# Mean of squares in a fused attention and gated feed-forward kernel: TensorE sums replaced by VectorE 32x32 transposes, once per two head pairs

## The chip, the cores and the metric

The kernel runs on one core of a Trainium2 chip. The metric is device time in microseconds for one execution. A core has TensorE (PE in the profile, its weight loads PEld), VectorE (DVE), ScalarE (ACT), GpSimd (POOL) and SyncE (SP), which here issues nearly all DMAs. Matmuls write to PSUM, which has eight banks of 128 partitions by 512 fp32.

## The reference

Two layers, one behind the other. First a linear attention with a root-mean-square norm over each head, then a feed-forward layer with a gate:

```python
kv  = einsum('bhsd,bhse->bhde', k, v)          # batch 8, heads 8, seq 576, head_dim 64
out = einsum('bhsd,bhde->bhse', q, kv)
x   = out / sqrt(mean(out * out, axis=-1) + 1e-6) * g_norm
x   = x.transpose(0, 2, 1, 3).reshape(4608, 512)
h   = x @ w_in                                  # 512 -> 2048
sp  = maximum(h, 0) + log1p(exp(-abs(h)))       # softplus
out = (h * erf(sp)) @ w_out                     # 2048 -> 512
```

The mean of squares is over the 64 values of one head, and that sum is what the change moves.

## The kernel before, in words

**Groups.** The 4608 tokens are worked in nine groups of 512, `T` = 0 to 8. Group `T` below 8 is the first 512 rows of batch entry `T`; the last 64 rows of each entry are gathered in the tile `x_last` and make up group 8. Tokens lie along the free dimension and the features of two heads on the 128 partitions, so a group's attention output is four tiles of 128x512, one for each pair of heads (`p` = 0 to 3). The sum over one head is thus a sum over 64 partitions.

**Stages.** Groups 0 to 2 get their attention in code of their own (`first_group`, and `attention` for groups 1 and 2) beside the set-up of the weights and the feed-forward of groups 0 and 1, which ends near 235 us. Then comes the main loop over `m` (line 1318), one iteration for each four hidden units of a group; a group has 16 units and so four iterations, `b` = 0 to 3. An iteration makes four hidden products (`hidden`), then the four result products of the iteration before (`result`). In the profile both have line 773, and are told apart by the tiles: `x_forms,w_in_parts` for hidden, `w_out_parts,g_forms` for result. Each is 12 matmuls of 128x128 by 128x512: every operand is kept in three forms (high, low, both), eight matmuls go to the bank `n_ps` and four to the bank `m_ps`. A pair of banks is taken from six in rotation (`pair_of_banks`); the other two hold `at_ps`, the attention output of the pair in work. The weights' forms are read from DRAM afresh in each group (line 1019, four tiles in and four out in each iteration), into a few buffers.

**What follows a product.** A hidden product: ScalarE copies `n_ps` to `h` (line 1367), VectorE adds `m_ps` (line 743, `h<-m_ps,h`), ScalarE makes softplus (line 1372) and, for all four units, erf (line 1395); VectorE multiplies (line 1421, "the gates") and the next iteration cuts the gates into three forms (lines 703, 706, 709, `g_forms`). A result product: VectorE adds `n_ps` (line 738) and `m_ps` (line 743, `e<-m_ps,e`) to the running sum, or in the first iteration of a group writes it (line 1304).

**The attention of the next group.** While group `T` is worked, each iteration `b` does pair `b` of group `T+1`, cut into pieces that are called at places of the iteration: place 0 is its start, place 1 to 4 follow the hidden products 0 to 3, place 5 to 8 the result products 0 to 3. The order of the work on each engine is the order in which the code issues it (the schedule is by hand). `paired` handles groups 3 to 7: in even `b` (`side` 0) the piece `visit` makes the products of two pairs on TensorE (lines 579 and 610). In each iteration follow: `square` on ScalarE (line 634, out of `at_ps`), `halve` on VectorE (lines 640 and 641: the squares in a rounded high part and a low part), `mean` (two matmuls with the constant `mean_w`, lines 645 and 646, into a bank of the rotation that `next_bank` gives, then the exp and log table, Ln, Exp with scale -0.5, Square, lines 650 to 652), `norm` on VectorE (a correction step in two 128x512 instructions, lines 658 and 661, and the product with the attention output and g, line 665), and the split into three forms `x_forms` (lines 703, 706, 709). `keep` copies the 64-row rest and the next pairs' k-v products out of PSUM (lines 621, 378, 380); `turns` transposes the next two q tiles in blocks of 32x32 (line 345). Group 8 runs through `attention` in its branch for `T == B`, with the same steps (lines 486, 487, 498 to 518).

ScalarE's functions come from tables that have to be loaded: erf, exp with log, and softplus are three of them (`ACT_TABLE_LOAD`, lines 112, 115, 1395).

Of the kernel before, what the change touches and what calls it, by code (L numbers as in the profile page):

```python
# [39 lines left out]
FP32 = mybir.dt.float32  # L40
# [2 lines left out]
U32 = mybir.dt.uint32  # L43
AF = mybir.ActivationFunctionType
ALU = mybir.AluOpType
PSUM = bass.MemoryType.PSUM

EPS = 1e-6
# [7 lines left out]
FIRST = 2  # L56
SHIFT = 4096.0
SQ = 32
ORDER = """
kv0 fill0 q0 fill1 q_out0 kv_out0 result0 kv1 kv_out1 q1 square0 q_out1 mean0 log0 result1 kv2 kv_out2  # L60
root0 tail square1 again0 tail_out mean1 kv3 log1 root1 q2 again1 q3 q_out2 norm_a0 norm_b0 kv_out3 norm_c0 q_out3
# [7 lines left out]
def kernel(  # L69
# [262 lines left out]
    def halves_of(t):  # L332
        return t.rearrange("p (a t) -> p a t", a=2)
# [65 lines left out]
        kept.pop()()  # L399
        turn(1, 0)  # L400

    def attention(T, p, in_parts=False):

        st = {}

        halves = T > 1 or (T == 1 and p > 0)
        quad = T < B
# [4 lines left out]
        def two(t):  # L412
            return halves_of(t) if quad else t

        bd = kv_of(T, p)

        def bank(name):
            if p == 0:
                at_pool(2)
            return ps_now[0].tile([P, G], FP32, name=name, tag="at")  # L420

        def square_tile(name):
            return qt_tile(name)[:, 0:G]
# [1 line left out]
        def visit():  # L425


            qT = ready.pop((T, p))
            at = st["at"] = at_tile()
            x = halves_of(qT[:, 0:G])  # L430
            for a, i in ((0, 0), (0, 1), (1, 0), (1, 1)):
                nc.tensor.matmul(  # L432
                    at[rows_of[i if a else 1 - i], a, 0 : 2 * P],
                    lhsT=bd[rows_of[i], a * D : (a + 1) * D],
                    rhs=x[rows_of[i], a],
                    start=True,
                    stop=True,
                )
# [5 lines left out]
            if then[0] < B:  # L444
                for _, product_ in kv_products(*then, at[:, 1, kv_cols], at[:, 0, kv_cols], first=1):
                    product_()  # L446
            if both:
                for _, product_ in kv_products(then[0], 1, at[:, 1, more_cols], at[:, 0, more_cols]):
                    product_()
            st["sq"] = qT[:, 0:G]  # L450
            nc.scalar.activation(two(st["sq"]), st["o"], AF.Square)

        def keep_tail():
            nc.vector.tensor_copy(
                out=x_last[:, p, T * R : T * R + R], in_=st["at"][:, 1, 2 * P : 2 * P + R]
            )
            if then[0] < B:
                kv_kept(*then, st["at"])
            if both:
                kv_kept(then[0], 1, st["at"], more_cols)  # L460

        def square():
            st["o"], st["sq"] = x_last[:, p, :], square_tile("sq")
            nc.scalar.activation(st["sq"], st["o"], AF.Square)

        def halve():
            sq = st.pop("sq")
# [3 lines left out]
            nc.vector.tensor_tensor(out=lo, in0=sq, in1=hi.bitcast(FP32), op=ALU.subtract)  # L471

        def mean(table=True):
            if quad:
                ms = st["at"][:, :, 2 * P : 4 * P]
                parts = [(ms[:, a], a) for a in range(2)]
            else:
                ms = bank("ms_ps")
                parts = [(ms, slice(0, G))]
            st["ms"] = ms  # L480
            if halves:


# [63 lines left out]
            if i == (FIRST + 1) * NP:  # L547
                load_kv(i + 1)

        after = (split_upper, split_lower) if in_parts else (split,)  # L550
        if T == B:
            return lambda: None, square, halve, mean, norm, *after
# [4 lines left out]
        return (*(partial(chain, *group) for group in pieces), mean, partial(chain, norm, then_), *after)  # L557


    twice = {}  # L560

    def paired(T, p, in_parts=False):

        i = T * NP + p
        u_tile = partial(attp.tile, [P, G], FP32, name="u", tag="sq_lo")
        side = p % 2
        if side == 0:
            twice.clear()
        st = {}

        def visit():

# [56 lines left out]
                )  # L629

        def square():
            st["o"] = twice["at"][:, :, side * 2 * P : (side + 1) * 2 * P]
            st["sq"] = x_new.tile([P, G], FP32, name="sq", tag="x")
            nc.scalar.activation(halves_of(st["sq"]), st["o"], AF.Square)

        def halve():
            sq = st.pop("sq")
            hi = st["hi"] = attp.tile([P, G], FP32R, name="sq_hi", tag="rms_r")
            lo = st["lo"] = attp.tile([P, G], FP32R, name="sq_lo", tag="sq_lo")
            nc.vector.tensor_copy(out=hi, in_=sq)  # L640
            nc.vector.tensor_tensor(out=lo, in0=sq, in1=hi.bitcast(FP32), op=ALU.subtract)

        def mean(table=True):
            ms = st["ms"] = next_bank("ms_ps")
            nc.tensor.matmul(ms, lhsT=mean_w, rhs=st.pop("hi"), start=True, stop=False)  # L645
            nc.tensor.matmul(ms, lhsT=mean_w, rhs=st.pop("lo"), start=False, stop=True)  # L646
            u = st["u"] = u_tile()
            r = st["r"] = attp.tile([P, G], FP32, name="rms_r", tag="rms_r")
            exp_ln_table()
            nc.scalar.activation(r, ms, AF.Ln, bias=eps_col)  # L650
            nc.scalar.activation(r, r, AF.Exp, scale=-0.5)
            nc.scalar.activation(u, r, AF.Square)
            if table:
                softplus_table()

        def norm():
            ms, u, r = (st.pop(name) for name in ("ms", "u", "r"))
            nc.vector.scalar_tensor_tensor(
                out=u, in0=ms, scalar=EPS, in1=u, op0=ALU.add, op1=ALU.mult
            )  # L660
            nc.vector.scalar_tensor_tensor(
                out=u, in0=u, scalar=3.0, in1=r, op0=ALU.subtract, op1=ALU.mult
            )
            x = st["x"] = x_new.tile([P, G], FP32, name="x", tag="x")
            nc.vector.scalar_tensor_tensor(
                out=halves_of(x),
                in0=st.pop("o"),
                scalar=gm_col,
                in1=halves_of(u),
                op0=ALU.mult,  # L670
                op1=ALU.mult,
            )

        def split_upper():
            upper(st["x"], x_forms[T][0][:, p])

        def split_lower():
            lower(st.pop("x"), *(form[:, p] for form in x_forms[T]))

        def q_loads():  # L680
            if i == (FIRST + 1) * NP:
# [9 lines left out]
            for n in range(2):  # L691
                turn(*divmod(i + 1 + n, NP))

        after = (split_upper, split_lower) if in_parts else (partial(chain, split_upper, split_lower),)
        if side == 0:
            start = (q_loads, partial(chain, visit, square, halve, keep, kv_loads), chain)
        else:
            start = (chain, partial(chain, square, halve), turns)
        return (*start, mean, norm, *after)

    def upper(x, high):

# [44 lines left out]
    def pair_of_banks(*names, turns=True):  # L747
# [5 lines left out]
            banks.extend(banks[:2])  # L753
            del banks[:2]
        return pair

    def next_bank(name):
        pool, tag = banks[0]
        banks.append(banks.pop(0))
        return pool.tile([P, G], FP32, name=name, tag=tag)  # L760

    def product(weights, moving, turns=True, cuts=()):

# [554 lines left out]
    for m in range(first_batch, batches + 1):  # L1318
# [1 line left out]
        todo = []  # L1320
        last_ = b == NB - 1 and T + 1 < NG
        if T + 1 < NG:
            todo = list((attention if T + 1 == B else paired)(T + 1, b, in_parts=last_))
            if b == 0:
                side = late_r if T % 2 == FIRST % 2 else late
                forms = side.tile([P, 3, KC, G], FP32R, name=f"x_forms{(T + 1) % 2}")
                x_forms[T + 1] = [forms[:, i] for i in range(3)]

        def piece():
            if todo:  # L1330
# [12 lines left out]
        def pieces(place):  # L1343
            while todo and places[-len(todo)] <= place:
                todo.pop(0)()

        def fetch(place):
            for which in FETCH[place].split():
# [112 lines left out]
```

## Time and profile before

| what | value |
|---|---|
| median of 3 runs | 896.05 us (896.02 to 896.56) |
| the profiled execution: time | 896.7 us |
| the profiled execution: span from first to last instruction | 894.9 us |
| granted TensorE clock, mean | 1.000 |
| busy PE / PEld / DVE / ACT | 886.7 / 668.5 / 761.0 / 594.9 us |
| HBM traffic | 224.40 MB read, 34.60 MB written, 289 GB/s over the span |
| lines 645 and 646, the mean's matmuls of groups 3 to 7 | 20 each, 392 and 393 ns |
| lines 640, 641, 658, 661, 665 on DVE | 20 each, 418, 693, 684, 691, 751 ns |
| lines 650, 651, 652 on ACT | 20 each, 690, 633, 633 ns |

A row of the profile names line, engine, operation, output and inputs with their shapes, count, then busy time and the mean duration of one, and the idle time in front of it with what ended it. Durations of instructions on one engine overlap a little, so that the distance from start to start is the better price of one. Matmuls are pipelined: one takes 390 ns from its start to its end, while the next starts 227 ns behind it.

### The profile page before, as it was taken

Reading aid. Unit: us, or ns where it says so; the run is one execution under the profiler, and the core shown is the slowest. Engines: PE = TensorE matmul, PEld = TensorE weight load, DVE = VectorE, ACT = ScalarE, POOL = GpSimd, SP = SyncE. Lnnn points to the kernel's source line nnn. Section 1 sums busy time; section 2 is a strip of 40 time slices with the busy share of each in tenths; the row PEclk is TensorE's granted clock in tenths of the full one; section 3 lists DMA queues with packets and bytes.
Section 4 is the critical chain, followed back from the end, with each engine's and each line's share of the span. In section 5 each row is a group of like instructions: output and inputs, shape, how many; then the busy total and the mean of one; then the engine's idle time right before and its main releaser. Section 6 shows DMA issues by size and latency. Waiting matters only on the chain.

```text
span 894.9 us, 13333 instructions
## 1 busy us (share of the span) xinstructions
PE 886.7 (99%) x4922; PEld 668.5 (75%) x4922; DVE 761.0 (85%) x1095; ACT 594.9 (66%) x789; POOL 4.7 (1%) x14
## 2 busy tenths in 40 slices
PE   8999999999999999999999999999999999999998
PEld 4444456666788888888888888888888888888887
DVE  5899979899889898989898989898988888886667
ACT  5976677777766666666666656565666766665552
POOL 2000000000000000000000000000000000000000
PEclk9999999999999999999999999999999999999999
DMA  9977418889799987998799879998887787778861
GB/s 288 296 226 226 112 74 315 314 337 351 258 351 397 307 334 249 404 288 339 258 367 342 342 219 350 359 337 271 291 326 274 286 313 300 283 286 319 316 261 50
DMA packets 136929, 259.89 MB, mean 290 GB/s; under 512 B 78816, under 2 KB 87264, under 8 KB 136864
## 3 DMA queue, kind: packets, MB, share of 16 engines
q1 hardware_dynamic: 136128, 258.09, 81.1%
q10 hardware_dynamic: 544, 0.82, 0.3%
q8 instruction: 39, 0.64, 0.3%
q14 instruction: 26, 0.21, 0.1%
q0 software_dynamic: 192, 0.13, 0.1%
HBM read 224.40 MB, written 34.60 MB: 289 GB/s over the span
## 4 chain that ended last, share of the span: by engine, by line
PE 91%; DMA 4%; DVE 3%; ACT 2%; issue 1%; SPq 0%; DVEq 0%; ACTq 0%
PE n_ps L773 48%; PE m_ps L773 24%; PE o_ps L829 8%; PE h_ps L1196 5%; DMA w_in_parts<-w_in 1%; DMA w_out_parts<-w_out 1%; PE at_ps L579 1%; PE off_ps L610 1%; DMA w_in<-w_new 1%; PE warm_ps L977 1%; PE ms_ps L646 1%; PE ms_ps L645 1%; PE at_ps L432 0%; PE at_ps L446 0%; DMA w_out<-w_place 0%
## 5 line engine op out<-in xcount | busy, mean ns | idle before, releaser
L773 PE MATMUL n_ps<-w_out_parts,g_forms 128*128 128x512 f32 (+1 forms) x936 | 230.4, 388 | 0.3 <-DMA w_out_parts<-w_out 0.3
L773 PE MATMUL n_ps<-x_forms,w_in_parts 128*128 128x512 f32 x896 | 222.7, 391 | 0.0
L773 PEld LDWEIGHTS n_ps<-w_out_parts,g_forms 128*128 128x128 f32 x936 | 175.1, 188 | 37.2 <-DMA w_out_parts<-w_out 0.7
L773 PEld LDWEIGHTS n_ps<-x_forms,w_in_parts 128*128 128x128 f32 x896 | 167.4, 188 | 35.1
L743 DVE TENSOR_TENSOR h<-m_ps,h 128x512 f32<-128x512 f32 x116 | 78.0, 686 | 60.9 <-PE m_ps L773 57.7
L773 PE MATMUL m_ps<-w_out_parts,g_forms 128*128 128x512 f32 x464 | 123.8, 389 | 0.0
L1372 ACT ACTIVATE s<-h 128x512 f32<-128x512 f32 x112 | 69.3, 631 | 79.0 <-DVE h L743 78.9
L773 PE MATMUL m_ps<-x_forms,w_in_parts 128*128 128x512 f32 x448 | 119.7, 389 | 0.0
L1367 ACT ACTIVATE h<-n_ps 128x512 f32<-128x512 f32 x112 | 66.0, 592 | 78.3 <-PE n_ps L773 77.1
L773 PEld LDWEIGHTS m_ps<-w_out_parts,g_forms 128*128 128x128 f32 x464 | 87.1, 188 | 18.1
L773 PEld LDWEIGHTS m_ps<-x_forms,w_in_parts 128*128 128x128 f32 x448 | 84.1, 188 | 17.5
L743 DVE TENSOR_TENSOR e<-m_ps,e 128x512 f32<-128x512 f32 x116 | 80.1, 692 | 15.3 <-PE m_ps L773 5.0
L829 PE MATMUL o_ps<-w_out_sb,h_sb 128*128 128x512 f32 x192 | 86.8, 595 | 0.0
L709 DVE SCALAR_TENSOR_TENSOR g_forms<-g_forms 128x1024 fp32r<-128x1024 f32 x58 | 71.1, 1225 | 2.0
L706 DVE TENSOR_TENSOR g_forms<-h,g_forms 128x1024 fp32r<-128x1024 f32 x58 | 70.5, 1216 | 0.5 <-ACT g_forms L703 0.4
L703 ACT ACTIVATE g_forms<-h 128x1024 fp32r<-128x1024 f32 x58 | 58.4, 1049 | 15.5 <-PE m_ps L773 11.1
L738 DVE SCALAR_TENSOR_TENSOR e<-n_ps,e 128x512 f32<-128x512 f32 (+1 forms) x89 | 60.3, 678 | 7.1 <-PE n_ps L773 7.1
L1421 DVE TENSOR_TENSOR h<-h,s 128x1024 f32<-128x1024 f32 x56 | 65.9, 1217 | 0.0
L829 PEld LDWEIGHTS o_ps<-w_out_sb,h_sb 128*128 128x128 f32 x192 | 35.5, 190 | 38.3 <-issue 36.9
L1196 PE MATMUL h_ps<-xT,w_in_sb 128*128 128x512 f32 x128 | 57.9, 596 | 1.3 <-DVE w_in_sb L290 1.2
L115 ACT ACT_TABLE_LOAD x43 | 55.2, 1283 | 0.8
L1395 ACT ACTIVATE s<-s 128x1024 f32<-128x1024 f32 x50 | 50.6, 1054 | 0.3
(175 smaller groups left out, 1014.0 us busy)
## 6 DMA issues: line engine op xcount, KB each, us to landing
w_out_parts<-w_out SPq DMA_DIRECT2D x116, 768.0 KB, 7.1
w_in_parts<-w_in SPq DMA_DIRECT2D x112, 768.0 KB, 6.6
w_in<-w_new SPq DMA_DIRECT2D x16, 768.0 KB, 4.8
k_sb<-in_k_dram SPq DMA_DIRECT2D x32, 288.0 KB, 5.6
v_sb<-in_v_dram SPq DMA_DIRECT2D x31, 288.0 KB, 5.7
w_raw<-in_moe_w_in_dram SPq DMA_DIRECT2D x16, 512.0 KB, 5.9
w_raw<-in_moe_w_out_dram SPq DMA_DIRECT2D x8, 1024.0 KB, 5.0
out_dram<-e SPq DMA_DIRECT2D x32, 256.0 KB, 3.5
```

Of the source, the lines that this page charges most:

```text
L115: nc.scalar.preload_act_table_set("softplus")
L703: nc.scalar.activation(high, x, AF.Copy, scale=1.0 + 2.0**-13)
L706: nc.vector.tensor_tensor(out=low, in0=x, in1=high.bitcast(FP32), op=ALU.subtract)
L709: nc.vector.scalar_tensor_tensor(out=both, in0=low.bitcast(FP32), scalar=SHIFT, in1=high.bitcast(FP32), op0=ALU.mult, op1=ALU.add,)
L738: nc.vector.scalar_tensor_tensor(out=out_, in0=ps, scalar=scale, in1=out_, op0=ALU.mult, op1=ALU.add)
L743: nc.vector.tensor_tensor(out=out_, in0=ps, in1=out_, op=ALU.add)
L773: nc.tensor.matmul(ps[:, cols], lhsT=weights(form, k), rhs=moving(form, k)[:, cols], start=(form == forms[0] and k == 0), stop=(form == fo ...
L829: nc.tensor.matmul(o_ps[j], lhsT=g[:, j * P : j * P + P], rhs=one(w_out_sb, f), start=(f == 0), stop=last,)
L1196: nc.tensor.matmul(plain[i], lhsT=blocks_of(one(w_in_sb, i % FC))[:, c], rhs=xT[T][:, c, :], start=(c == 0), stop=(c == KC - 1),)
L1367: nc.scalar.activation(h[:, i], n_ps, AF.Copy, scale=SHIFT - 1.0)
L1372: nc.scalar.activation(s[:, i], h[:, i], AF.Softplus)
L1421: nc.vector.tensor_tensor(out=part(h, half), in0=part(h, half), in1=part(s, half), op=ALU.mult)
```

## The change

In groups 3 to 8 the mean of squares leaves TensorE. One set of pieces now serves two pairs, in even `b`: both squares are taken at once (with scale 0.125, so that the square is already divided by 64); VectorE transposes each 128x512 tile of squares in blocks of 32x32 and sums each block along the free dimension, which leaves 128x16 for a pair, 128x32 for both; ScalarE copies the four quarters of 32 partitions crosswise and VectorE adds them, since a head covers two quarters; Ln, Exp and Square run on 128x32; the correction step runs on 128x32; and a transpose of the column, read with stride 0, spreads the factor back to 128x512. The product with g follows for both pairs at place 8, the split at places 1 to 3 of the odd iteration, the transposes of the next q at its place 5 (before: place 3). `halve`, `mean` and `next_bank` are gone from this path, the exp and log table is loaded in even `b` only, and group 8 goes through the same pieces, reading `x_last`. The tiles of squares and of x are now of the tag that the transposed q has.

```diff
-    def attention(T, p, in_parts=False):
+    def attention(T, p):
...
         def square():
-            st["o"] = twice["at"][:, :, side * 2 * P : (side + 1) * 2 * P]
-            st["sq"] = x_new.tile([P, G], FP32, name="sq", tag="x")
-            nc.scalar.activation(halves_of(st["sq"]), st["o"], AF.Square)
-
-        def halve():
...
-        def mean(table=True):
-            ms = st["ms"] = next_bank("ms_ps")
-            nc.tensor.matmul(ms, lhsT=mean_w, rhs=st.pop("hi"), start=True, stop=False)
-            nc.tensor.matmul(ms, lhsT=mean_w, rhs=st.pop("lo"), start=False, stop=True)
...
+            xs = twice["x"] = [qt_tile("x")[:, 0:G] for _ in range(2)]
+            for n, x in enumerate(xs):
+                if T == B:
+                    o = x_last[:, p + n]
+                else:
+                    o, x = twice["at"][:, :, n * 2 * P : (n + 1) * 2 * P], halves_of(x)
+                twice["o", n] = o
+                nc.scalar.activation(x, o, AF.Square, scale=0.125)
+
+        def small(name):
+            t = twice[name] = attp.tile([P, 2 * BLOCKS], FP32, name=name, tag=name)
+            return t
+
+        def block_sums():
+            total = small("ms")
+            for n in range(2):
+                t = attp.tile([P, G], FP32, name="sq_t", tag=("rms_r", "sq_lo")[n])
+                nc.vector.transpose(out=t, in_=twice["x"][n])
+                nc.vector.tensor_reduce(
+                    out=total[:, n * BLOCKS : n * BLOCKS + BLOCKS],
+                    in_=t.rearrange("p (c d) -> p c d", c=BLOCKS),
+                    axis=AX.X,
+                    op=ALU.add,
+                )
+
+        def across():
+            total, other = twice["ms"], small("ms_other")
+            for n in range(4):
+                rows, beside = (slice(32 * k, 32 * k + 32) for k in (n, n ^ 1))
+                nc.scalar.copy(other[rows], total[beside])
+            nc.vector.tensor_tensor(out=total, in0=total, in1=other, op=ALU.add)
+
+        def root():
+            total, r, u = twice["ms"], small("rms"), small("rms_u")
             exp_ln_table()
-            nc.scalar.activation(r, ms, AF.Ln, bias=eps_col)
+            nc.scalar.activation(r, total, AF.Ln, bias=eps_col)
             nc.scalar.activation(r, r, AF.Exp, scale=-0.5)
             nc.scalar.activation(u, r, AF.Square)
...
+        def spread():
+            total, r, u = (twice[name] for name in ("ms", "rms", "rms_u"))
             nc.vector.scalar_tensor_tensor(
-                out=u, in0=ms, scalar=EPS, in1=u, op0=ALU.add, op1=ALU.mult
+                out=u, in0=total, scalar=EPS, in1=u, op0=ALU.add, op1=ALU.mult
             )
             nc.vector.scalar_tensor_tensor(
                 out=u, in0=u, scalar=3.0, in1=r, op0=ALU.subtract, op1=ALU.mult
             )
+            for n in range(2):
+                nc.vector.transpose(
+                    out=twice["x"][n].rearrange("p (c d) -> p c d", c=BLOCKS),
+                    in_=u[:, n * BLOCKS : n * BLOCKS + BLOCKS].unsqueeze(2).to_broadcast([P, BLOCKS, 32]),
+                )
...
         if side == 0:
-            start = (q_loads, partial(chain, visit, square, halve, keep, kv_loads), chain)
+            first = {0: (q_loads,), 2: (visit, square, keep, kv_loads)} if T < B else {0: (square,)}
+            norms = [partial(norm, n) for n in range(2)]
+            pieces = first | {3: (block_sums,), 4: (across,), 5: (root,), 6: (spread,), 8: norms}
         else:
-            start = (chain, partial(chain, square, halve), turns)
-        return (*start, mean, norm, *after)
+            pieces = {
+                1: [partial(split_upper, n) for n in range(2)],
+                2: (partial(split_lower, 0),),
+                3: (partial(split_lower, 1),),
+                5: (turns,),
+            }
+        return sorted((place, partial(chain, *some)) for place, some in pieces.items())
...
-            todo = list((attention if T + 1 == B else paired)(T + 1, b, in_parts=last_))
+            todo = paired(T + 1, b)
...
-        places = (0, 2, 3, 5, 6, 8)
-        if T + 1 == B:
-            places = (0, 0, 2, 5, 7, 8)
-        if last_:
-            places = (0, 0 if T + 1 == B else 2, 2 if T + 1 == B else 3, 4, 5, 5, 6)
-            todo[3] = partial(todo[3], table=False)
-
         def pieces(place):
-            while todo and places[-len(todo)] <= place:
-                todo.pop(0)()
+            while todo and todo[0][0] <= place:
+                todo.pop(0)[1]()
...
-            if len(todo) < 2:
+            if not last_ and (b % 2 or not todo):
                 softplus_table()
```

More of the change, by code (lines that the diff above doesn't have):

```diff
@@ L45 @@
 ALU = mybir.AluOpType
+AX = mybir.AxisListType
 PSUM = bass.MemoryType.PSUM
@@ L58 @@
 SQ = 32
+BLOCKS = 16
 ORDER = """
@@ L400, in keep_prepared @@
         turn(1, 0)
-    def attention(T, p, in_parts=False):
+    def attention(T, p):
         st = {}
         halves = T > 1 or (T == 1 and p > 0)
-        quad = T < B
         then = divmod(T * NP + p + 1, NP)
@@ L410, in attention @@
         more_cols = slice(kv_cols.stop, kv_cols.stop + D)
-        def two(t):
-            return halves_of(t) if quad else t
+        two = halves_of
         bd = kv_of(T, p)
[L417 to L420, printed above, removed]
         def square_tile(name):
@@ L443, in visit @@
             st["o"] = at[:, :, 0 : 2 * P]
-            if then[0] < B:
-                for _, product_ in kv_products(*then, at[:, 1, kv_cols], at[:, 0, kv_cols], first=1):
-                    product_()
+            for _, product_ in kv_products(*then, at[:, 1, kv_cols], at[:, 0, kv_cols], first=1):
+                product_()
             if both:
@@ L456, in keep_tail @@
             )
-            if then[0] < B:
-                kv_kept(*then, st["at"])
+            kv_kept(*then, st["at"])
             if both:
                 kv_kept(then[0], 1, st["at"], more_cols)
-        def square():
-            st["o"], st["sq"] = x_last[:, p, :], square_tile("sq")
-            nc.scalar.activation(st["sq"], st["o"], AF.Square)
         def halve():
@@ L473, in mean @@
         def mean(table=True):
[L474 to L480, printed above, removed]
+            ms = st["ms"] = st["at"][:, :, 2 * P : 4 * P]
+            parts = [(ms[:, a], a) for a in range(2)]
             if halves:
@@ L548, in loads @@
                 load_kv(i + 1)
-        after = (split_upper, split_lower) if in_parts else (split,)
-        if T == B:
-            return lambda: None, square, halve, mean, norm, *after
         first_ = (partial(prepare, T, p),) if (T, p) == (1, 0) else ()
@@ L556, in attention, with paired @@
         pieces = (first_, (visit, loads), (halve, keep_tail) if halves else (keep_tail,))
-        return (*(partial(chain, *group) for group in pieces), mean, partial(chain, norm, then_), *after)
+        return (*(partial(chain, *group) for group in pieces), mean, partial(chain, norm, then_), split)
     twice = {}
-    def paired(T, p, in_parts=False):
+    def paired(T, p):
         i = T * NP + p
-        u_tile = partial(attp.tile, [P, G], FP32, name="u", tag="sq_lo")
         side = p % 2
@@ L568, in paired @@
             twice.clear()
-        st = {}
         def visit():
@@ L631, in square @@
         def square():
-            st["o"] = twice["at"][:, :, side * 2 * P : (side + 1) * 2 * P]
-            st["sq"] = x_new.tile([P, G], FP32, name="sq", tag="x")
-            nc.scalar.activation(halves_of(st["sq"]), st["o"], AF.Square)
-        def halve():
[L637 to L641, printed above, removed]
@@ L643, in mean @@
-        def mean(table=True):
-            ms = st["ms"] = next_bank("ms_ps")
[L645 to L648, printed above, removed]
+            xs = twice["x"] = [qt_tile("x")[:, 0:G] for _ in range(2)]
[6 more added lines that the diff above has]
+                nc.scalar.activation(x, o, AF.Square, scale=0.125)
@@ L651, in mean @@
             nc.scalar.activation(r, r, AF.Exp, scale=-0.5)
             nc.scalar.activation(u, r, AF.Square)
[L653 to L657, printed above, removed]
+            softplus_table()
+        def spread():
+            total, r, u = (twice[name] for name in ("ms", "rms", "rms_u"))
             nc.vector.scalar_tensor_tensor(
-                out=u, in0=ms, scalar=EPS, in1=u, op0=ALU.add, op1=ALU.mult
+                out=u, in0=total, scalar=EPS, in1=u, op0=ALU.add, op1=ALU.mult
@@ L663, in norm, with split_upper, split_lower @@
             )
-            x = st["x"] = x_new.tile([P, G], FP32, name="x", tag="x")
-            nc.vector.scalar_tensor_tensor(
[L666 to L671, printed above, removed]
-            )
[L674 to L678, printed above, removed]
+            for n in range(2):
[3 more added lines that the diff above has]
+                )
+        def norm(n):
+            x = twice["x"][n]
+            if T < B:
+                x = halves_of(x)
+            nc.vector.scalar_tensor_tensor(
+                out=x, in0=twice["o", n], scalar=gm_col, in1=x, op0=ALU.mult, op1=ALU.mult
+            )
+        def split_upper(n):
+            upper(twice["x"][n], x_forms[T][0][:, p - side + n])
+        def split_lower(n):
+            lower(twice["x"][n], *(form[:, p - side + n] for form in x_forms[T]))
         def q_loads():
@@ L692, in turns @@
                 turn(*divmod(i + 1 + n, NP))
-        after = (split_upper, split_lower) if in_parts else (partial(chain, split_upper, split_lower),)
         if side == 0:
-            start = (q_loads, partial(chain, visit, square, halve, keep, kv_loads), chain)
-        else:
-            start = (chain, partial(chain, square, halve), turns)
-        return (*start, mean, norm, *after)
+            first = {0: (q_loads,), 2: (visit, square, keep, kv_loads)} if T < B else {0: (square,)}
+            norms = [partial(norm, n) for n in range(2)]
+            pieces = first | {3: (block_sums,), 4: (across,), 5: (root,), 6: (spread,), 8: norms}
+        else:
+            pieces = {
[5 more added lines that the diff above has]
+        return sorted((place, partial(chain, *some)) for place, some in pieces.items())
     def upper(x, high):
@@ L755, in pair_of_banks @@
         return pair
[L757 to L760, printed above, removed]
     def product(weights, moving, turns=True, cuts=()):
@@ L1327 @@
                 x_forms[T + 1] = [forms[:, i] for i in range(3)]
-        def piece():
-            if todo:
-                todo.pop(0)()
-        places = (0, 2, 3, 5, 6, 8)
-        if T + 1 == B:
-            places = (0, 0, 2, 5, 7, 8)
-        if last_:
-            places = (0, 0 if T + 1 == B else 2, 2 if T + 1 == B else 3, 4, 5, 5, 6)
-            todo[3] = partial(todo[3], table=False)
         def pieces(place):
-            while todo and places[-len(todo)] <= place:
-                todo.pop(0)()
+            while todo and todo[0][0] <= place:
+                todo.pop(0)[1]()
         def fetch(place):
```

## The prediction

> **What bounds the kernel now.** I read the engine shares first, then the waits of TensorE, then the busy time by stage, and last the instructions in order of time where the step sits. The stretch that matters starts at 240 us, where the main loop begins.
>
> Engine shares of the page, and the chain that ended last, by engine:
>
> ```profile
> PE 886.7 (99%) x4922; PEld 668.5 (75%) x4922; DVE 761.0 (85%) x1095; ACT 594.9 (66%) x789; POOL 4.7 (1%) x14
> ...
> PE 91%; DMA 4%; DVE 3%; ACT 2%; issue 1%; SPq 0%; DVEq 0%; ACTq 0%
> ```
>
> The only waits of TensorE: of its weight loads from 290 to 850 us, and of its matmuls from 250 us to the end (what waited, for whom, us in total, times, longest):
>
> ```profile
> PEld at_ps L579 <- issue: 2.8, 8, 0.4
> ```
> ```profile
> PE n_ps L773 <- DMA w_out_parts<-w_out: 0.3, 1, 0.3
> ```
>
> TensorE waits for nobody in the main loop, so whatever leaves its queue shortens the loop, unless a new wait fills the hole. Two stages (two visits apart, one iteration pair each), with VectorE as the nearest competitor:
>
> ```profile
> 337.40:384.30 46.90, 46.90 (x293) 38.59 (x293) 41.32 (x59) 31.08 (x42) 0.00 (x0) 1.00 0.91 327
> 384.30:431.20 46.90, 46.90 (x293) 38.59 (x294) 41.51 (x60) 30.87 (x41) 0.00 (x0) 1.00 0.89 309
> ```
>
> The columns are the stretch, its length, busy PE, PEld, DVE, ACT, POOL, then the granted clock and the DMA share. PE fills all 46.9 us at clock 1.00; DVE has 5.5 us free, ACT 15.9. Now the step itself on TensorE:
>
> ```profile
> 409.29 1.98 PE L773 MATMUL n_ps<-x_forms,w_in_parts 128*128 128x512 f32 x8
> 411.10 1.07 PE L773 MATMUL m_ps<-x_forms,w_in_parts 128*128 128x512 f32 x4
> 412.01 0.39 PE L645 MATMUL ms_ps<-sq_hi,mean_w 128*128 128x512 f32 x1
> 412.24 0.39 PE L646 MATMUL ms_ps<-sq_lo,mean_w 128*128 128x512 f32 x1
> 412.47 2.00 PE L773 MATMUL n_ps<-w_out_parts,g_forms 128*128 128x512 f32 x8
> 415.21 1.98 PE L773 MATMUL n_ps<-w_out_parts,g_forms 128*128 128x512 f32 x8
> ```
>
> A product (12 matmuls) takes 2.72 us start to start (409.29 to 412.01). The two mean matmuls hold TensorE from 412.01 to 412.47, and the product behind them takes 2.74 us: a mean costs 0.46 + 0.02 = 0.48 us.
>
> **Part 1, TensorE loses the means.** The tile's view counts L645/L646 twenty times and L486/L487 on a full bank four times, 24 pairs in all (the first three groups keep theirs). 24 x 0.48 = 11.5 us, all on the path that sets the end. Nothing else covers it: no wait of PE lies at these places. The profiled execution took 896.7 us with a span of 894.9; the median of the runs is 896.05. The gain is a difference of TensorE occupancy and applies to either: 896.05 - 11.5 = 884.5 us.
>
> **Part 2, VectorE.** Start to start, from the stage at 384 us: removed per pair are the cast to sq_hi 0.45, the subtraction 0.61, and two wide normalisation steps (L658, L661) 0.71 and 0.73, together 2.50, so 5.00 per two pairs. Added per two pairs: two 128x512 transposes with a 512 to 16 sum each, one 128x32 addition, two 128x32 steps, two 128x512 transposes of a broadcast column. No row shows the sum or the broadcast, so I bound them: below, the cast at 0.42; above, a 1024-element step at 1.22. The nearest rows are the one-element-a-cycle forms:
>
> ```profile
> L345 DVE STREAM_TRANSPOSE qT<-q_sb 128x576 f32<-128x576 f32 x28 | 20.6, 759 | 1.4 <-DMA v_sb<-in_v_dram 1.4
> L661 DVE SCALAR_TENSOR_TENSOR u<-u,rms_r 128x512 f32<-128x512 f32 x20 | 13.8, 691 | 0.7
> L640 DVE CAST sq_hi<-sq 128x512 fp32r<-128x512 f32 x20 | 8.4, 418 | 0.7 <-ACT sq L634 0.7
> ```
>
> From 512 elements at 0.691 to 1024 at 1.225 (L709) is 1.04 ns an element; at 576 that line gives 0.758, and the transpose reads 759 ns, so a transpose runs at this pace and I take 0.69 for all six (0.72 start to start behind its own producer, 0.61 otherwise). At 32 elements the line gives 0.19; the 128x128 step reads 0.28, which is the upper end. Sum: 2 x (0.72 + 0.61) + 0.20 + 2 x 0.22 + 0.72 + 0.61 = 4.63. VectorE gains 0.37 per two pairs: 41.4 becomes 41.0 of a stage that shrinks to 45.94, 89%. A rule of the Trainium skill speaks against the change: the page "VectorE: DVE Perf Modes", section "Rules for kernel authors", calls tensor_reduce the slowest VectorE operation and advises restructuring it off a hot path. The same page's fp32 formula, elements plus 151 at 0.96 GHz, makes an estimate of 0.69 us for 512 elements; by it the sum stays 4.63, and no run here has timed the sum yet.
>
> **Part 3, ScalarE.** Per two pairs it loses two each of Ln 0.69, Exp 0.63 and Square 0.63 (3.90) and a table load (1.28): the exp and log table is loaded in one iteration of two instead of in each. It gains four 32-row copies and three 128x32 functions. ACT at 512 takes 0.629 and at 1024 1.049 (L703), so the line gives 0.24 at 32 elements; bounds 0.1 and 0.6, value 0.24: 7 x 0.24 = 1.7. Net 3.5 us less on an engine with 15.9 us free: no time.
>
> **Part 4, order and lag.** Six banks hold three products, so a product's evacuation must end before the third product behind it starts. (The mean's own bank goes too, which only loosens this.) The latest evacuation is the hidden unit 0 of the odd iteration, behind the gates, the normalisation, two result evacuations and the cut of the gates:
>
> ```profile
> 343.15 0.69 DVE L743 TENSOR_TENSOR h<-m_ps,h 128x512 f32<-128x512 f32 x1 [2.03 <-PE m_ps L773]
> 343.75 1.22 DVE L706 TENSOR_TENSOR g_forms<-h,g_forms 128x1024 fp32r<-128x1024 f32 x1
> 349.60 2.35 DVE L1421 TENSOR_TENSOR h<-h,s 128x1024 f32<-128x1024 f32 x2
> 358.09 1.22 DVE L706 TENSOR_TENSOR g_forms<-h,g_forms 128x1024 fp32r<-128x1024 f32 x1
> 360.49 1.28 DVE L743 TENSOR_TENSOR h<-m_ps,h 128x512 f32<-128x512 f32 x2
> 362.40 1.98 PE L773 MATMUL n_ps<-x_forms,w_in_parts 128*128 128x512 f32 x8
> ```
>
> Before: the addition ends at 361.17, TensorE needs the bank at 362.40, 1.2 us to spare (0.9 in the stage at 407.74). After, on the same clock: the addition of unit 2 starts at 340.43, block sums run 341.04 to 343.70, addition 3 ends its slot at 344.30, the cut at 346.70, the 128x32 addition 346.90, results 0 and 1 at 349.69, gates 2.27 to 351.96, the two small steps 352.40, spread 353.73, results 2 and 3 356.52, both multiplications by g 357.86 (the second pair's moved here from the odd iteration), cut 360.26, addition 0 ends 360.94. TensorE needs it at 362.40 - 0.48 = 361.92: 1.0 to spare, by the other stage some 0.6. The 2.03 us in which VectorE stood idle is what hides the block sums. If that cover were gone, their 2.66 would land on this path. Result 2 reads the cut that now ends at 346.95 and starts at 348.3, 1.4 to spare.
>
> New waits: the four ScalarE copies wait for the sums with the erf table behind them, and the sums end before ScalarE's softplus of unit 3 does, so nothing is held. The 128x32 addition on VectorE waits for the copies with the result evacuations behind it; softplus ends at about 345.0, the copies at 346.0, before 346.7. Ln, Exp, Square then end near 351.4, before VectorE asks at 351.96. In the odd iteration the splits move from places 5 to 8 into the hidden units and the q transposes from place 3 to 5; there the sums of VectorE give addition 0 of the next iteration 2.1 us after its product, against an allowance of 5.4. The next group's operands are ready 10 us earlier than now (the last split ends at 421.9, read at 423.4).
>
> **DMA.** SP's queue keeps its order; only the q tiles come free two places later, and their next loads are issued in the next iteration. TensorE asks for weights 0.48 us earlier per iteration. From the trace's landings, a weight tile waits at least 2.9 us for its first matmul from 290 us on; around 250 to 275 us the slack is 0.04, 1.4 and 2.5 us at DMA shares above 1.0. The saving of the first two means may wait there: 0 to 1 us. I take 0.
>
> **Rivals.**
> A, forecast: TensorE stays full, 884.5 us. Own range 884 to 888.
> B, small stalls: each of the nine new VectorE instructions 0.15 longer than taken, 1.35 per stage, less a slack of 0.6 to 1.0, is 0.35 to 0.75 lost in each of 12 stages, 4 to 9 us: 889 to 893.5. For: the slack is under 1 us. Against: the transpose row fits the line to 1 ns.
> C, slower: VectorE becomes the bound through the six wide new operations. At 1.22 each they add 6 x 0.53 = 3.2 us; less 0.8 slack, 2.4 us per stage, 29 us in 12 stages: 884.5 + 29 = 913. It decides from 0.8 + 0.96 = 1.8 us per stage, that is from 0.99 us for each. For: no row has a reduction or a stride-0 read. Against: every one-element-a-cycle form here reads 0.68 to 0.69.
> D, the weights are the limit: a stage cannot shrink below its DMA share. The largest share after 290 us is 0.96 of 46.9, 45.0, under 45.94, so the price is the early 1 us; only if 0.91 were the true ceiling would nothing be gained, 896.
>
> **How the numbers follow.** A 0.74, B 0.13, C 0.09, D 0.04 (no change). A change under 0.2% (1.8 us) is about what a measurement of this kernel can't tell from none. Faster 0.87, same 0.04, slower 0.09. The range leaves out C, D and the upper end of B: 883.5 (the low end is A less 1 us, twice the 0.5 between the runs of before) to 892.
>
> **What would show it.** Right: no PE row for ms_ps after 240 us, stages of 45.9 us with PE still filled, a sum and a transpose near 0.69, DVE near 41 a stage, no new PE wait on DVE. Wrong: PE waiting for the additions at L743's counterpart near the odd iteration's start, a wide new operation above 0.9 us, or PE waiting for w_in_parts or w_out_parts in the steady stages.

## The result and the profile after

The changed kernel takes 884.99 us (884.54 to 885.67), the kernel before 896.25 us with the runs of the same comparison: a ratio of 0.9875, 95% interval 0.9858 to 0.9892, 11.3 us less. The forecast was 884.5. The span fell from 894.9 to 883.2 us, 11.7 less. One run of dose 3 below took 1263.52 us at a granted TensorE clock of 0.655 (0.999 to 1.000 in all others) and is left out, with its profile, the only one of that dose.

From the page after, engine shares and the chain by engine, and the waits of TensorE's matmuls and weight loads in the main loop, from 240 us on (columns: what waited, for whom, us in total, times, longest):

```profile
PE 875.1 (99%) x4874; PEld 659.1 (75%) x4874; DVE 752.6 (85%) x1107; ACT 559.3 (63%) x789; POOL 4.7 (1%) x14
...
PE 91%; DMA 3%; DVE 2%; ACT 2%; issue 1%; SPq 0%; DVEq 0%; ACTq 0%
```
```profile
PE n_ps L778 <- DMA w_out_parts<-w_out: 0.2, 1, 0.2
```
```profile
PEld at_ps L557 <- issue: 3.5, 10, 0.4
PEld n_ps L778 <- DMA w_out_parts<-w_out: 0.9, 2, 0.6
```

The row with "issue", time in which nothing is waited for that the profile shows, comes with the ten visits; the kernel before has it too (3.5 us). PE's busy time is 11.6 us lower with 48 matmuls fewer, its share is 99% as before, and no wait on VectorE or ScalarE has come up in the main loop. Two stages, with busy PE, PEld, DVE, ACT and POOL:

```profile
335.20:381.10 45.90, 45.90 (x296) 37.83 (x288) 40.61 (x60) 28.12 (x41) 0.00 (x0) 1.00 0.93 330
381.10:427.10 46.00, 46.00 (x298) 37.84 (x289) 40.71 (x60) 27.99 (x41) 0.00 (x0) 1.00 0.95 320
```

A stage, from one hidden unit 2 behind a visit to the next, runs from 335.22 to 381.15, 45.93 us where it was 46.9, and PE fills it. On TensorE the result products now follow each other at 2.72 us with nothing in between:

```profile
340.79 1.98 PE L778 MATMUL n_ps<-w_out_parts,g_forms 128*128 128x512 f32 x8
342.60 1.07 PE L778 MATMUL m_ps<-w_out_parts,g_forms 128*128 128x512 f32 x4
343.51 1.98 PE L778 MATMUL n_ps<-w_out_parts,g_forms 128*128 128x512 f32 x8
```

The new operations, by shape (busy us, mean ns of one, idle time before):

```profile
L629 DVE STREAM_TRANSPOSE sq_t<-x 128x512 f32<-128x512 f32 x24 | 16.8, 702 | 0.0
L630 DVE TENSOR_REDUCE ms<-sq_t 128x16 f32<-128x512 f32 x24 | 16.5, 686 | 0.8
L665 DVE STREAM_TRANSPOSE x<-rms_u 128x512 f32<-128x512 f32 x24 | 15.7, 691 | 0.4
L643 ACT COPY ms_other<-ms 32x32 f32<-32x32 f32 x48 | 10.3, 215 | 0.7
L649 ACT ACTIVATE rms<-ms,eps_col 128x32 f32<-128x32 f32 x12 | 3.9, 322 | 0.1
```

The sum and the stride-0 read, which had no row before, take 686 and 691 ns, as long as the additions of 512 fp32 elements (L743 before, 686 to 692 ns). Last, VectorE through the stretch that the prediction worked out, and the product of TensorE at its end:

```profile
338.34 0.69 DVE L753 TENSOR_TENSOR h<-m_ps,h 128x512 f32<-128x512 f32 x1 [1.19 <-PE m_ps L778]
338.95 0.70 DVE L629 STREAM_TRANSPOSE sq_t<-x 128x512 f32<-128x512 f32 x1
...
341.63 0.68 DVE L753 TENSOR_TENSOR h<-m_ps,h 128x512 f32<-128x512 f32 x1
342.23 1.21 DVE L716 TENSOR_TENSOR g_forms<-h,g_forms 128x1024 fp32r<-128x1024 f32 x1
...
344.62 0.18 DVE L644 TENSOR_TENSOR ms<-ms,ms_other 128x32 f32<-128x32 f32 x1
...
349.77 0.18 DVE L658 SCALAR_TENSOR_TENSOR rms_u<-ms,rms_u 128x32 f32<-128x32 f32 x1
349.99 0.19 DVE L661 SCALAR_TENSOR_TENSOR rms_u<-rms_u,rms 128x32 f32<-128x32 f32 x1
350.22 1.30 DVE L665 STREAM_TRANSPOSE x<-rms_u 128x512 f32<-128x512 f32 x2
351.44 0.65 DVE L748 SCALAR_TENSOR_TENSOR e<-n_ps,e 128x512 f32<-128x512 f32 x1
...
354.20 1.40 DVE L674 SCALAR_TENSOR_TENSOR x<-at_ps,gm_col,x 128x512 f32<-128x512 f32 x2
357.91 1.28 DVE L753 TENSOR_TENSOR h<-m_ps,h 128x512 f32<-128x512 f32 x2
...
359.83 1.98 PE L778 MATMUL n_ps<-x_forms,w_in_parts 128*128 128x512 f32 x8
```

The block sums stand where VectorE used to be idle for 2.03 us, and in this stretch only its first instruction follows a wait. There is no wait for ScalarE in it: neither the small addition (344.62) nor the first small step (349.77) has one.

### The profile page after: what moved, and what is told of

Same layout as the page of the kernel before. It is cut to its first block, busy times and chain, and to the rows that moved or that the text cites. A ratio compares the mean times of both kernels' runs of the same rounds, so it can differ in the third digit from the quotient of the medians.

```text
span 883.2 us, 13286 instructions
## 1 busy us (share of the span) xinstructions
PE 875.1 (99%) x4874; PEld 659.1 (75%) x4874; DVE 752.6 (85%) x1107; ACT 559.3 (63%) x789; POOL 4.7 (1%) x14
## 4 chain that ended last, share of the span: by engine, by line
PE 91%; DMA 3%; DVE 2%; ACT 2%; issue 1%; SPq 0%; DVEq 0%; ACTq 0%
PE n_ps L778 48%; PE m_ps L778 24%; PE o_ps L834 8%; PE h_ps L1201 5%; DMA w_out_parts<-w_out 1%; PE at_ps L557 1%; DMA q_sb<-in_q_dram 1%; PE off_ps L588 1%; DMA w_in<-w_new 1%; PE warm_ps L982 1%; DMA w_in_parts<-w_in 0%; PE at_ps L427 0%; ACT s_sb L1154 0%; PE at_ps L440 0%; ACT L1154 0%
## 5 line engine op out<-in xcount | busy, mean ns | idle before, releaser
L713 ACT ACTIVATE g_forms<-h 128x1024 fp32r<-128x1024 f32 x58 | 60.8, 1061 | 39.2 <-PE m_ps L778 21.0
```

The source lines that it names most:

```text
L713: nc.scalar.activation(high, x, AF.Copy, scale=1.0 + 2.0**-13)
```

## The experiments

Theory T: the gain is the time that TensorE no longer spends on the means, and nothing else. Its rivals: the shorter work of VectorE or ScalarE makes it (V, S). For how far VectorE's new work is from the limit: a lag of 1.24 us (L), no limit below full occupancy (F), no room at all (G), and later N.

**The changed kernel again.**

> The changed kernel once more, as the base of the runs beside it: 885.0 us, 11.2 less than before.

884.78 us (884.18 to 885.11), ratio 0.9866 (0.9852 to 0.9881). With the first comparison the base is 884.9 us.

**TensorE's two matmuls put back, unread.**

```diff
+        def idle_mean():
+            pool, tag = banks[0]
+            banks.append(banks.pop(0))
+            ps = pool.tile([P, G], FP32, name="idle_ps", tag=tag)
+            for c in range(2):
+                nc.tensor.matmul(
+                    ps, lhsT=mean_w, rhs=x_forms[T - 1][0][:, c], start=(c == 0), stop=(c == 1)
+                )
...
-            pieces = first | {3: (block_sums,), 4: (across,), 5: (root,), 6: (spread,), 8: norms}
+            pieces = first | {3: (block_sums,), 4: (across,), 5: (idle_mean, root), 6: (spread,), 8: norms}
...
-                5: (turns,),
+                5: (idle_mean, turns),
```

> The changed kernel with two matmuls per pair put back at place 5, of the mean's size and weights and into the next bank of the rotation; their result is read by nobody. Theory T (the whole gain is the time TensorE no longer spends on the means): 24 x 0.48 = 11.5 us come back, 896.5 us. Rival V (the gain comes from VectorE's and ScalarE's shorter chain, or from fewer waits on them, and TensorE's matmuls lay in a hole): 885 to 887 us.

896.61 us (895.75 to 897.16), ratio to the kernel before 0.9999 (0.9990 to 1.0008): the whole gain is gone. TensorE in order of time, and the engine shares of the page:

```profile
344.88 1.07 PE L787 MATMUL m_ps<-w_out_parts,g_forms 128*128 128x512 f32 x4
345.79 0.62 PE L703 MATMUL idle_ps<-x_forms,mean_w 128*128 128x512 f32 x2
346.25 2.00 PE L787 MATMUL n_ps<-w_out_parts,g_forms 128*128 128x512 f32 x8
```
```profile
PE 887.2 (99%) x4922; PEld 668.7 (75%) x4922; DVE 753.8 (84%) x1107; ACT 559.6 (63%) x789; POOL 4.7 (1%) x14
```

The idle pair holds TensorE for 0.46 us, as the mean did, while DVE and ACT keep the lower times of the changed kernel (753.8 and 559.6). VectorE's and ScalarE's relief is worth nothing by itself. V is out. (The idle pair also takes a bank of the rotation again; the next run leaves the bank in use and takes away only a matmul.)

**One of the two matmuls left out of the kernel before.** The low part of the squares is made but not added.

```diff
-            nc.tensor.matmul(ms, lhsT=mean_w, rhs=st.pop("hi"), start=True, stop=False)
-            nc.tensor.matmul(ms, lhsT=mean_w, rhs=st.pop("lo"), start=False, stop=True)
+            nc.tensor.matmul(ms, lhsT=mean_w, rhs=st.pop("hi"), start=True, stop=True)
```

(the same in the four pairs of group 8)

> The kernel before with only the first of the mean's two matmuls in groups 3 to 8 (the low part of the squares is still made but not added to the mean). VectorE's and ScalarE's work is that of before. Theory T: 24 x 0.227 = 5.4 us less than before, 890.7 us. Rival V: 896 us, no change.

891.34 us (890.07 to 891.73), ratio 0.9938 (0.9923 to 0.9953) to 896.55 beside it: 5.2 us less, against 24 x 0.227 = 5.4, with nothing changed on ScalarE and nothing taken from VectorE. The same price from the other side.

**ScalarE's work put back.**

```diff
             softplus_table()
+            for _ in range(6):
+                nc.scalar.copy(twice["t", 0], twice["t", 1])
```

(in `root`; `twice["t", n]` are the tiles `sq_t` of `block_sums`)

> The changed kernel with six 128x512 copies (about 3.6 us) added on ScalarE per two pairs, behind the softplus table load of place 5, about what the change took off this engine. Theory T (ScalarE's relief gives no time): 885.0 to 885.5 us. Rival S (the relief of ScalarE is part of the gain, since the cut of the gates now starts sooner): each stage loses at least 0.5 us, 891 us or more.

885.0 us (884.76 to 885.54), ratio 0.9869 (0.9852 to 0.9885). ACT's busy time is 596.1 us, more than the 594.9 of the kernel before. In its trace the six copies run from 351.22 and the cut of the gates follows at 355.01 at once, where it came at 350.68 in the changed kernel and at 354.64 in the kernel before; no wait of TensorE's matmuls appears in the main loop. S is out.

**VectorE's work raised in steps.** The transpose in front of the block sums is done again, in total one to six times more per two pairs (shown for dose 1; the counts for the two tiles are 2 and 1, then 2 and 2, 3 and 2, 3 and 3, and 4 and 4 for dose 6):

```diff
-                nc.vector.transpose(out=t, in_=twice["x"][n])
+                for _ in range(2 if n == 0 else 1):
+                    nc.vector.transpose(out=t, in_=twice["x"][n])
```

> The changed kernel with one more 128x512 transpose on VectorE per two pairs, in front of the block sums (the same transpose done twice). In the changed kernel's trace the latest evacuation, that of hidden unit 0 of the odd iteration, ends 1.24 us before TensorE needs its bank in nearly every stage. Theory L (that lag is VectorE's limit): 0.6 to 0.7 us fit in, 885.0 us. Rival F (VectorE's share of 88% leaves 5 us per stage, lag is no limit): 885.0 us. Rival G (no room at all): 12 x 0.65 = 7.8 us, 893 us.

> Two more transposes per two pairs, 1.2 to 1.4 us. Theory L: 0 to 0.2 us over the room of 1.24, times 12 stages, 885 to 887.5 us. Rival F: 885.0 us. Rival G: 900 us.

> Four more transposes per two pairs, 2.4 to 2.9 us. Theory L: 1.2 to 1.6 us per stage are lost, 12 stages, 899 to 905 us, slower than the kernel before; TensorE's matmuls then wait for VectorE's addition of a hidden unit. Rival F: 885.0 us, since 5 us per stage are free. Rival G: 915 us.

Doses 1 and 2 cost nothing (884.99 and 885.13 us; ratios 0.9866, 0.9852 to 0.9881, and 0.9869, 0.9855 to 0.9884), so G is out. Dose 4 takes 896.49 us, ratio 0.9994 (0.9985 to 1.0004): the gain is gone, so F falls, but by less than L said. In its trace a repeated transpose costs 0.745 us (three from 341.02 to the sum at 343.25), so dose 2 is 1.49 us, 0.25 over L's room. At this price L would lose 12 x 0.25 = 3 us at dose 2, 888 us, and misses it as well; its recorded range, worked out with a shorter transpose, still held 885.13. The waits of dose 4, first of the matmuls, then of the weight loads:

```profile
PE n_ps L779 <- DVE e L749: 4.5, 11, 0.4
PE n_ps L779 <- DMA w_out_parts<-w_out: 1.2, 3, 0.5
```
```profile
PEld n_ps L779 <- DVE e L749: 9.6, 12, 0.9
PEld at_ps L557 <- issue: 3.5, 10, 0.4
PEld n_ps L779 <- DVE g_forms L717: 3.1, 11, 0.3
PEld n_ps L779 <- DMA w_out_parts<-w_out: 3.1, 5, 1.0
```

L749 is the evacuation of a result's `n_ps`, not of the hidden unit's `m_ps` on which L stood. The order of time shows why. VectorE's evacuation of result 2's `n_ps` and TensorE's hidden units 0 and 1:

```profile
356.51 0.66 DVE L749 SCALAR_TENSOR_TENSOR e<-n_ps,e 128x512 f32<-128x512 f32 x1
```
```profile
353.94 1.98 PE L779 MATMUL n_ps<-x_forms,w_in_parts 128*128 128x512 f32 x8
355.75 1.07 PE L779 MATMUL m_ps<-x_forms,w_in_parts 128*128 128x512 f32 x4
357.21 2.11 PE L779 MATMUL n_ps<-x_forms,w_in_parts 128*128 128x512 f32 x8 [0.40 <-DVE e L749]
```

Hidden unit 1 starts at 357.21, 0.04 us behind the end of that evacuation (357.17), and 3.27 us behind unit 0 instead of 2.72. A product writes `n_ps` for 1.81 us before it touches `m_ps`, so the two banks have different dates, and the addition of `m_ps` has 1.8 us more than L gave it. Theory N: in the changed kernel the first limit is result 2's `n_ps`, free at 352.09 and needed by hidden unit 1 at 354.39, 2.3 us:

```profile
354.39 1.98 PE L778 MATMUL n_ps<-x_forms,w_in_parts 128*128 128x512 f32 x8
356.20 1.07 PE L778 MATMUL m_ps<-x_forms,w_in_parts 128*128 128x512 f32 x4
```

Two more doses were to tell:

> The changed kernel with three more transposes per two pairs, 3 x 0.745 = 2.24 us by the rows of the doses before. Theory L (room 1.24 us, up to the start of the third product behind hidden unit 0): 1.0 lost in each of 12 stages, 897 us. Theory N (the bank m_ps is written only after eight matmuls, 1.8 us later, so the first limit is result 2's n_ps, which is free 2.3 us before hidden unit 1 of the odd iteration needs it): 2.24 fits, 885 to 886 us.

> Six more transposes per two pairs, 6 x 0.745 = 4.47 us. Theory L: 3.2 lost per stage, 923 us. Theory N: 4.47 - 2.3 = 2.2 lost per stage, 26 us, 911 us, with TensorE waiting for the evacuation of result 2's n_ps and for the cut of the gates.

Dose 3 takes 887.32 us, ratio 0.9895 (0.9879 to 0.9912); dose 6 takes 913.7, ratio 1.0190 (1.0175 to 1.0205). L's 897 and 923 are out. N is right in kind and some 0.2 to 0.3 us too wide (it missed dose 3's 885 to 886 by 1.3 us, and dose 6's 911 by 2.7): the loss per stage, (time - 884.9) / 12, is 0.01, 0.02, 0.20, 0.97 and 2.40 us at 0.75, 1.49, 2.24, 2.98 and 4.47 us of added work, close to a straight line from 2.0 us on. That result 2 also meets the cut of the gates shows in dose 6, where it is the longer wait. Its weight loads, and the two matmuls of one stage that follow a wait:

```profile
PEld n_ps L779 <- DVE g_forms L717: 21.1, 12, 1.8
PEld n_ps L779 <- DVE e L749: 10.0, 12, 0.9
```
```profile
352.23 1.89 PE L779 MATMUL n_ps<-w_out_parts,g_forms 128*128 128x512 f32 x7 [1.36 <-DVE g_forms L717]
360.89 2.11 PE L779 MATMUL n_ps<-x_forms,w_in_parts 128*128 128x512 f32 x8 [0.42 <-DVE e L749]
```

The traces let the two be taken apart. A steady stage lasts 45.93 us in the changed kernel and at doses 1 and 2, 46.82 at dose 4 and 48.32 at dose 6: 0.89 and 2.39 us lost, which leaves a room of 2.1 us at both doses. At dose 4, 0.20 us of the 0.89 come from result 2 and the cut, 0.55 from hidden unit 1's late start and 0.14 from its longer run (`n_ps` to `m_ps`, 357.21 to 359.17, 1.96 us against 1.81); at dose 6 it is 1.67, 0.58 and 0.15. The longer run is the larger part of what N left out. The rest of the loss in dose 4's trace lies in four longer stages, the four in which weight loads also wait for DMA (3.1 us in all).

**The same step in groups 1 and 2.** In the seven pairs of `attention` that had the rounded halves, pair by pair:

```diff
-            nc.vector.tensor_copy(out=hi, in_=sq)
-            nc.vector.tensor_tensor(out=lo, in0=sq, in1=hi.bitcast(FP32), op=ALU.subtract)
+            nc.vector.transpose(out=t, in_=st["sq"])
+            nc.vector.tensor_reduce(
+                out=total, in_=t.rearrange("p (c d) -> p c d", c=BLOCKS), axis=AX.X, op=ALU.add
+            )
...
-                for ps, a in parts:
-                    nc.tensor.matmul(ps, lhsT=mean_w, rhs=hi[:, a], start=True, stop=False)
-                    nc.tensor.matmul(ps, lhsT=mean_w, rhs=lo[:, a], start=False, stop=True)
+                for n in range(4):
+                    rows, beside = (slice(32 * k, 32 * k + 32) for k in (n, n ^ 1))
+                    nc.scalar.copy(other[rows], total[beside])
+                nc.vector.tensor_tensor(out=total, in0=total, in1=other, op=ALU.add)
...
+                nc.vector.transpose(
+                    out=u.rearrange("p (c d) -> p c d", c=BLOCKS),
+                    in_=column_.unsqueeze(2).to_broadcast([P, BLOCKS, 32]),
+                )
```

> The changed kernel with the same replacement, pair by pair, in the seven pairs of groups 1 and 2 that had the rounded halves (28 matmuls of 128x256 gone from TensorE between 100 and 240 us). Theory T: 7 x 0.5 = 3.5 us less than the changed kernel, 881.5 us. Rival W (there VectorE is 89% busy and the small addition has to wait for ScalarE's copies in the order of its queue): the gain is taken back, 885 to 888 us.

882.7 us (882.18 to 883.14), ratio 0.9841 (0.9827 to 0.9856): 2.2 us below the base where T said 3.5. Set beside the changed kernel's trace, TensorE's products come 0.38 to 0.49 us earlier at each of six pairs, 2.8 in all, and 0.7 is given back near 124 us. VectorE, and TensorE from 90 to 245 us:

```profile
117.88 0.18 DVE L472 TENSOR_TENSOR ms<-ms,ms_other 128x16 f32<-128x16 f32 x1 [1.53 <-ACT ms_other L471]
```
```profile
PE o_ps L1113 <- DVE g_held L734: 0.7, 1, 0.7
PE o_ps L849 <- DVE h_sb L1097: 0.4, 1, 0.4
PE n_ps L1113 <- ACT e L1144: 0.2, 1, 0.2
```

Here the small addition does wait for ScalarE's copies, as rival W said, and what is queued behind it on VectorE is late; the gates (L1097) then hold TensorE for 0.4 us, near 124 us. The seventh pair, near 222 us, gains nothing: TensorE's next products wait there for VectorE's cut `g_held`, 0.4 us in the changed kernel and 0.7 here, and another 0.2 us is given back. One more run took the copies to VectorE, beside the same kernel again:

```diff
-                    nc.scalar.copy(other[rows], total[beside])
+                    nc.vector.tensor_copy(out=other[rows], in_=total[beside])
```

> The kernel more_groups with the four crosswise copies on VectorE in place of ScalarE (32x16 each, below 0.18 us). Theory W (what more_groups fell short of its 3.5 us is VectorE's wait of 5.3 us for ScalarE's copies): that wait goes, and about 1 us with it, 881.5 us. Rival X (the rest was lost elsewhere, or VectorE's added copies cost as much as the wait): 882.7 us or more.

> The kernel more_groups again, beside more_groups_v on the same chip: 882.7 us.

882.75 us (882.24 to 883.05) and 883.26 us (882.85 to 883.7), ratios 0.9842 (0.9827 to 0.9857) and 0.9850 (0.9834 to 0.9866). W's 881.5 us is missed and X's 882.7 or more is met, but the traces hold something of both. VectorE's wait for the copies is gone from the trace, and of the 0.7 us near 124 us only 0.2 is left: counted from the matmuls at 7 us, TensorE is 2.62 us ahead of the changed kernel at 196 us, where the two runs of `more_groups` are 2.06 and 2.07 ahead. So W's wait was worth 0.55 us up to there, and what is left of the shortfall lies elsewhere, as X said, the seventh pair above all. The times can't show the 0.55 us, since their intervals overlap: TensorE's first 7 us alone differ by up to 0.9 us between these traces. Both lie below the changed kernel: no run of the two above 883.7, none of the changed kernel below 884.18.

## Why the prediction was right, and where not

**TensorE, 11.5 us.** Right: 11.3 between the medians, 11.7 between the spans, and the stage came out at 45.93 against 45.94. Putting the two matmuls back gives the old time to 0.01%, taking one away gives close to half the gain (5.2 us): this term is the whole result, and the mechanism is the one forecast.

**VectorE's sum, 4.63 us.** Right: the block sums took 338.95 to 341.63, 2.68 against 2.66; the small addition 0.10 start to start (0.20 assumed); the two small steps and the spread 1.67 against 1.77; together 4.45. DVE's share of a stage is 40.6 to 40.7 us, 41.0 forecast. The warning of the Trainium skill ("VectorE: DVE Perf Modes", section "Rules for kernel authors") that tensor_reduce is the slowest VectorE operation is not borne out at this size: 686 ns, while the transpose in front of it takes 702. The 0.69 us of the prediction, by its rows and by its estimate from the page's formula alike, came out to 2%.

**ScalarE, no time.** Right, and shown by the six copies. The relief was 2.9 us of a stage against 3.5 forecast. The small operations are not what is missing: they came at 0.22 to 0.32 us for 0.24, 1.64 together against 1.7, and the durations of all ScalarE instructions together fell by 41.0 us, 3.4 a stage. Busy time counts overlapping instructions once and fell by 35.6: behind the change the instructions overlap less.

**Order and lag.** The order was right, the limit wrong. The dates came out as worked (addition 0 ends at 358.59, 1.24 us before the start of the third product; 1.0 was said), but the step "a product's evacuation must end before the third product behind it starts" gave both banks one date. The `m_ps` bank is due 1.8 us later, and the tightest event is result 2's `n_ps`. The 1.4 us that result 2 was given behind the cut were also too few: dose 6 shows its matmuls going on when the cut's first step on VectorE is done, and in the changed kernel that step ends at 343.44, 2.8 us before result 2 starts. VectorE had 2.0 us of room in a stage, not 0.6 to 1.0. That this error cost nothing is due to its direction: the true room was the larger one. Rival B's price (0.35 to 0.75 per stage from 1.35 us of added work) was therefore too high: 1.49 us, put in front of the block sums, cost nothing. Rival C's point of decision was put at 1.8 us per stage, 0.99 us for each wide operation. The doses put it at 2.0 + 0.94 (the gain, 11.3 / 12) = 2.9 us, which is 0.69 + 2.9 / 6 = 1.18 us for each, just under the upper bound of 1.22. Dose 4 (2.98 us) met that point: 896.49 against 896.60 beside it. At the bound C adds 3.2 us, and by the doses' line that costs 12 x 1.2 = 14 us, 899 and not 913.

**DMA.** Right: 0 to 1 us was allowed near 250 to 275 us and the waits there are 0.9 us of weight loads, 0.2 of matmuls. In the later stages of that trace TensorE never waits for weights.

## What to carry to other kernels

Where one engine is full and its trace shows no wait, as here in the main loop, the price of a step on it is the shift of the next product's start, and it came back as a gain one for one, because the engine that inherits the work had gaps just where it arrives. Where TensorE already waited behind the step, as at the seventh pair near 222 us, the step was worth nothing. How much the inheriting engine can take is not its free share (5 us of a stage here) but the earliest date that a later product sets (2.0 us); read that date for each bank separately, from when the product first writes it. Repeating a harmless instruction in growing doses found that room, and where it ends, in five runs.

## What the runs showed of the hardware that was not expected

A repeated 128x512 transpose into the same tile costs 0.745 us start to start (dose 4), where the two independent ones that spread the factor follow at 0.61. A product that had to wait is slower to get through as well: from its first `n_ps` matmul to its first `m_ps` matmul it took 1.96 us (waiting for its bank) to 1.99 us (waiting for the cut) against 1.81. The bank is not the reason alone: the product behind a visit's small matmuls takes 1.94 too (335.22 to 337.16 in the changed kernel), with no wait shown. On 128x32, Ln takes 322 ns on ScalarE where Exp and Square take 232 and 229; it alone reads its bias from a column (`eps_col`), and no run here tells the function from the column.
